# Sines and exponentials by three groups in turn, with a third buffer for their arguments, and the order of all tasks searched anew

## The chip, the core and the metric

The kernel runs on one core of one Trainium2 chip. The metric is the time of one execution on the device in microseconds (us). The engines are named as the profile names them: PE (TensorE, matrix products into PSUM; PEld are its weight loads), DVE (VectorE), ACT (ScalarE, which evaluates functions from a loaded table), POOL (GpSimd) and SP (SyncE, which here only issues DMAs). Each engine runs its own instructions in order and waits for others by semaphores.

## The reference

A gate mixes two branches over the same input x (2048 positions, 640 channels):

```python
g = _sigmoid((x * gate_w).sum(-1, keepdims=True))
a = _A_ref(x, A_wqkv, A_wo)
b = _B_ref(x, B_A_re, B_A_im, B_B_re, B_B_im, B_C_re, B_C_im, B_log_dt, B_Dskip)
return g * a + (1 - g) * b
```

Branch A is attention with 32 heads of 20 channels, in which a position looks at 8 positions, 2 apart: q, k and v are x @ wqkv, then a softmax over 8 products of q with k, the weighted sum of v, and a product with wo. Branch B is a state space model with 192 complex states for each of 640 channels. Its convolution kernel is a sum of complex exponentials,

```python
P = jnp.exp(logdA[:, :, None] * l[None, None, :])
K = jnp.einsum("dn,dnl,dn->dl", Cc, P, dB).real
```

over 2048 positions l, and K is convolved with x by Fourier transforms of twice the length.

## The kernel before

One program holds both branches; its instructions are interleaved so that PE, DVE and ACT all have work.

**Order.** The program is written as tasks (`pl.add`), each with an engine or a choice of engines, what it depends on, and the slots it takes and gives back. The order in which tasks are written out, and the engine of each that has a choice, stand in a long string of numbers, `ORDER["main"]` for everything up to the Fourier transform of K and `ORDER["tail"]` for the rest. It was found by a search. An engine's instructions stand in the program in this order and run in it.

**The generator of K** (`KGen`). The 640 channels are taken in ten groups (c = 0 to 9). Of each group, a complex exponential is made from sines and real exponentials of arguments that are linear in l, factored over l. PE makes the arguments (tile `ar`, two buffers in PSUM) from the group's parameters (`L`, the arguments' left side) and a constant (`Rarg`). ACT makes three units of sines for a group (three instructions each) and three units of exponentials (two instructions each) into rings of slots: five slots for sines (`trg`), six for exponentials (`exq`), both parts of the tile `big`, but for one slot in `bufA`. DVE multiplies a unit's sines and exponentials (two instructions to `pt`, one to `qq`, which gives the slots back), and PE sums the products over states (`kps`). A copy to `E` ends a group; after group 4 and group 9 DVE spreads half of K out (`X`), and SP and POOL store it to DRAM (`Kx`) and load it back (`kc`).

Sines and exponentials need different tables in ACT; changing the table is an instruction of its own (ACT_TABLE_LOAD). Before, the groups go in the order sines of 0, exponentials of 0 and 1, sines of 1 and 2, exponentials of 2 and 3, and so on: two of a kind in turn. `L` has two buffers, group c in buffer c mod 2, and the load of group c (eight small DMAs on SP; for group 0 four of them on ACT) waits for the arguments of group c - 2. The parameters behind L (`Sprm` in DRAM) are stored piece by piece from `pc`, by SP or POOL. POOL clears the L buffers at the start.

**Attention** runs in eight rounds of 256 positions (0 to 7). DVE multiplies q with shifted k (`prod`, five instructions of 128 x 2048), PE sums them (`lg`), DVE takes a maximum (`mx`, `hi`, `lo`), ACT an exponential (`at` from `lg`, with the table of exponentials), PE a sum, DVE the quotient (`rs`, `at`). SP stores it to DRAM (`aS`) and loads it back in another layout (`asb`). POOL loads v's window (`vc`). DVE multiplies v with the weights (`pv`, five instructions of 128 x 2048), PE sums (`tb`), a copy goes to `oT`, PE multiplies with wo, and a scaled copy (`ga`) is stored (`gaS`). The copies out of PSUM (`oT`, `ga`, projections to `qA`, `kA`, `prj`, `vst`, `pv`; `big` and `bufA` from `bp` and `tb`) can run on ACT or DVE, as the order says.

**The rest.** Fourier transforms of x (`Usb` to `big`) and of K (`kc` to `bufA`) are products on PE (`bp`), whose results ACT or DVE copy out. The tail multiplies the spectra (`fp`, copies to `sp_u` and `sp_k`, then DVE's `ta`, `tc`, `Y`), transforms back (`cp`, `yp`) and mixes with branch A (`tt`, `ot`).

Of the kernel before, what the change touches and what calls it, by code (L numbers as in the profile page):

```python
# [11 lines left out]
ALU = mybir.AluOpType  # L12
# [8 lines left out]
S = 2048  # L21
# [19 lines left out]
def _attn_consts():  # L41
# [49 lines left out]
), "tail": (  # L91
# [442 lines left out]
HC = NCH // 2  # L534
CH = 2 * HC * CQ

# [223 lines left out]
class KGen:  # L760
    def __init__(self, cst, pre, tc, prm):
        self.tc, self.nc, self.prm = tc, tc.nc, prm
        nc = tc.nc
        self.Lb = []
        for i in range(2):
            L = pre.tile([128, 2, 2, 2 * NST], BF16, name=f"L{i}", tag="PHI", bufs=3)
            nc.gpsimd.memset(L[:], 0.0)
            for g2 in range(2):
                nc.gpsimd.memset(L[64 * g2:64 * g2 + 2], 1.0)
            self.Lb.append(L)  # L770
        self.R = cst.tile([128, SW + EW], BF16, name="Rarg")
        nc.gpsimd.dma_start(self.R[:], nc.inline_tensor(_arg_consts(), name="c_rarg").ap())
        self.S12 = cst.tile([128, 2, 128], BF16, name="S12")
        nc.gpsimd.dma_start(self.S12[:], nc.inline_tensor(_shift_consts(), name="c_s12").ap())
# [10 lines left out]
    def load_L(self, c, gs=(0, 1)):  # L785
        L = self.Lb[c % 2]
# [8 lines left out]
    def plan(self, pl, pa, pk, hold, params, opened, fin):  # L795
        nc, R = self.nc, self.R
        SCL = float(2.0 * np.pi / 65536.0)
        argt, prevarg, prevact, prevkmm, fins, ns = [], None, None, None, [], 0
        self.pqs, self.lastargs = [], argt
        for c in range(NCH):  # L800
            L = self.Lb[c % 2]
            if c:
                Lt = [pl.add(f"L{c}", "S", 5.2, lambda _, c=c: self.load_L(c), deps=argt[c - 2] if c > 1 else params, dma=1.3)]
            else:
                Lt = [pl.add(f"L0{e}", e, d, lambda _, g=g: self.load_L(0, (g,)), deps=params, dma=0.65) for g, e, d in ((0, "S", 1.5), (1, "A", 1.7))]
            argt.append([])
            ends, held = {}, {}
            b = {"started": set()}
            for kind in (0, 1) if c % 2 == 0 else (1, 0):
                for u in range(3):  # L810
                    ends[u, kind] = []
                    for gp in range(2):
                        for sub in ((0, 1) if gp == 0 else (0,)) if kind == 0 else (None,):
                            def args(_, u=u, kind=kind, gp=gp, sub=sub, b=b, L=L):
                                ar = b["ar"] = pa.tile([128, 2, 512], F32, name="ar")
# [619 lines left out]
```

## Time and profile before

| | us |
|---|---|
| runs (three) | 320.24, 322.25, 322.69 |
| median of the runs | 322.25 |
| the profiled execution | 319.85 |
| its span, first to last instruction | 318.1 |
| ACT busy, of the span | 290.8 |
| DVE busy | 289.6 |
| PE busy | 289.2 |

The profile describes one execution; its own time is below all three runs, and sums from it are made against 319.85 us. A row of the timeline reads: start, length, engine, line, operation, what is written from what, shapes, count, and in brackets the idle time ahead and what ended it. An engine with a q behind its name (SPq, ACTq) is its queue of DMA issues, and a length there is the time of issuing, not of the transfer. Rows of groups read: line, engine, operation, tiles, shapes, count | busy us in all, mean ns of one | idle us ahead. Rows of stages read: start:end, length, and the busy us of PE, PEld, DVE, ACT and POOL with their counts of instructions, then the granted clock, the share of DMA and GB/s. Instructions of ACT and DVE that follow one another overlap a little, so that a row's start to the next row's start is what an instruction takes from its engine's time.

### The profile page before, as it was taken

The page shows a single profiled execution, that of the slowest core. Times are in us where ns is not written, and L with a number is a line of the kernel's source. Part 1 is how long each engine was busy: PE and PEld are TensorE (multiplying, and loading weights), DVE is VectorE, ACT ScalarE, POOL GpSimd, SP SyncE. Part 2 cuts the span into 40 slices and gives each one's busy share as a digit, 9 for nine tenths or more (in the row PEclk, how much of TensorE's full clock was granted, in tenths as well). Part 3 has the DMA queues.
Part 4 walks back from the last instruction along what each step waited for, and adds up shares of the span by engine and source line. Part 5 has one row for each costly group of instructions (what it writes and reads, how often), then busy time and mean ns, then how long its engine had stood idle before and what let it go on. Part 6 is the DMA issues. An engine that isn't in the chain of part 4 may idle for free. (4 is left out here: it accounts for less than half of the span.)

```text
span 318.1 us, 12105 instructions
## 1 busy us (share of the span) xinstructions
PE 289.2 (91%) x5276; PEld 171.2 (54%) x5276; DVE 289.6 (91%) x401; ACT 290.8 (91%) x431; POOL 57.4 (18%) x87
## 2 busy tenths in 40 slices
PE   8899989989999999999988999989989999997860
PEld 3545543445555454546454555546657776667740
DVE  4999989999899999999999999998867799999891
ACT  3999959998999999999999999998998999997891
POOL 8710211551000001111032122030020000000063
PEclk9999999999999999999999999978999999997995
DMA  8994655574612114534687696751195436874057
GB/s 254 365 251 116 167 157 113 139 149 117 130 19 68 34 45 112 135 64 128 218 222 187 130 231 144 132 126 35 46 313 205 154 116 187 184 144 68 2 140 194
DMA packets 48494, 45.67 MB, mean 144 GB/s; under 512 B 28490, under 2 KB 42106, under 8 KB 48442
## 3 DMA queue, kind: packets, MB, share of 16 engines
q1 hardware_dynamic: 42088, 27.17, 33.5%
q0 software_dynamic: 5392, 17.01, 20.9%
q8 instruction: 41, 0.67, 0.9%
q10 hardware_dynamic: 962, 0.73, 0.9%
q14 instruction: 11, 0.09, 0.1%
HBM read 29.57 MB, written 14.01 MB: 137 GB/s over the span
## 5 line engine op out<-in xcount | busy, mean ns | idle before, releaser
L316 PE MATMUL tb<-bufA 128*128 128x512 bf16 x300 | 75.5, 383 | 2.6 <-ACT bufA L513 1.3
L843 ACT ACTIVATE big<-ar 128x740 bf16<-128x740 int16 (+1 forms) x72 | 57.2, 859 | 0.9 <-PE ar L828 0.6
L828 PE MATMUL ar<-Rarg,L 64*128 64x212 bf16 (+4 forms) x600 | 48.2, 255 | 4.2 <-ACT big L843 1.6
L845 ACT ACTIVATE big<-ar 128x848 bf16<-128x848 f32 x60 | 50.2, 909 | 0.2 <-PE ar L828 0.2
L316 PEld LDWEIGHTS <-bufA 128*128 128x128 bf16 x300 | 31.5, 120 | 29.4 <-issue 9.6
L455 DVE TENSOR_TENSOR pv<-vc,asb 128x2048 bf16<-128x2048 bf16 x40 | 47.3, 1216 | 0.0
L828 PEld LDWEIGHTS <-L 64*128 64x128 bf16 x600 | 20.8, 95 | 34.1 <-issue 31.1
L865 DVE TENSOR_TENSOR pt<-big 128x1024 bf16<-128x1024 bf16 x48 | 32.2, 700 | 0.5 <-ACT big L843 0.5
L883 PEld LDWEIGHTS <-pt 128*32 128x32 bf16 (+1 forms) x2560 | 23.1, 92 | 13.3 <-issue 10.9
L883 PE MATMUL kps<-qq,pt 128*32 128x21 bf16 (+1 forms) x2560 | 28.0, 175 | 1.5 <-issue 1.5
L486 PE MATMUL tb<-wo_sb,oT 128*128 128x320 bf16 x160 | 27.7, 301 | 0.0
L381 DVE TENSOR_TENSOR prod<-qA,kA 128x2048 bf16<-128x2048 bf16 x20 | 23.7, 1216 | 0.4 <-PE lg L387 0.4
L381 DVE TENSOR_TENSOR prod<-prj 128x2048 bf16<-128x2048 bf16 x20 | 23.8, 1217 | 0.0
L462 PE MATMUL tb<-pv,ind 128*64 128x512 bf16 (+1 forms) x192 | 22.6, 359 | 1.2 <-DVE prj L515 1.1
L513 ACT ACTIVATE sp_u<-fp 128x640 bf16<-128x640 f32 x31 | 22.0, 811 | 0.7 <-PE fp L1096 0.7
L867 DVE TENSOR_TENSOR qq<-big 128x1344 bf16<-128x1344 bf16 x24 | 21.2, 882 | 0.0
L513 ACT ACTIVATE sp_k<-fp 128x640 bf16<-128x640 f32 x30 | 21.0, 819 | 0.0
L374 POOL DMA_DIRECT2D vc<-vS x16 | 11.6, 729 | 50.4 <-DVE pv L455 36.4
L1214 POOL DMA_DIRECT2D out_dram<-ot x14 | 7.7, 558 | 69.3 <-PE yp L1187 67.2
L1096 PEld LDWEIGHTS <-PHI 128*128 128x128 bf16 x160 | 15.6, 97 | 7.7 <-issue 0.9
L486 PEld LDWEIGHTS <-oT 128*128 128x128 bf16 x160 | 13.3, 98 | 7.4 <-issue 3.2
L513 ACT ACTIVATE big<-bp 128x1024 bf16<-128x1024 f32 x15 | 15.0, 1044 | 2.1 <-PE bp L1327 2.1
(177 smaller groups left out, 539.9 us busy)
## 6 DMA issues: line engine op xcount, KB each, us to landing
vc<-vS POOLq DMA_DIRECT2D x16, 327.5 KB, 5.5
gaS<-ga SPq DMA_DIRECT2D x8, 320.0 KB
Usb<-in_A_x_dram POOLq DMA_DIRECT2D x8, 320.0 KB, 5.3
gaF<-gaS SPq DMA_DIRECT2D x8, 320.0 KB
bufA<-in_A_wqkv_dram SPq DMA_DIRECT2D x3, 800.0 KB
L<-Sprm SPq DMA_DIRECT2D x76, 30.0 KB
asb<-aS SPq DMA_DIRECT2D x16, 128.0 KB
psi<-c_psi SPq DMA_DIRECT2D x4, 512.0 KB
```

The lines of the kernel that those rows point to most:

```text
L316: nc.tensor.matmul(ppf, self.wq[:, which, kt, e::5], self.xT[:, c0 // 1024, kt, c0 % 1024:c0 % 1024 + SC], start=(kt == 0), stop=(kt == NK ...
L381: nc.vector.tensor_tensor(b[e][:], q[:, e, o:o + C].unsqueeze(1).to_broadcast([128, W, C]), win(k[:, e, :], o, W, DIL, C), ALU.mult)
L455: nc.vector.tensor_tensor(o, vw, b["asb"][:].unsqueeze(2).to_broadcast(sh), ALU.mult)
L462: nc.tensor.matmul(b["op", e][64 * a:64 * a + 64, 0:n, :], ind[:, 32:96], b["pv", e][:, w, a, 0:n, :], start=(w == 0), stop=(w == 3), skip ...
L486: nc.tensor.matmul(apf[:, :320], b["oT"][:, e, i * 128:(i + 1) * 128], wo_sb[:, e, hf * 320:(hf + 1) * 320], start=(e == 0), stop=(e == 4))
L513: nc.scalar.activation(o, i, ACT.Identity)
L828: nc.tensor.matmul(ar[:, g2, a0:a0 + ncol], L[rows, sb, gv, l0:l0 + 128], R[rows, c0:c0 + ncol], start=True, stop=True, tile_position=(64 ...
L843: nc.scalar.activation(d_[:, :, s0 * QW:s1 * QW], ar[:].bitcast(I16)[:, :, 0:2 * (s1 - s0) * QW:2], ACT.Sin, scale=SCL)
L845: nc.scalar.activation(dst[:, gp::2].rearrange("p g s n -> p g (s n)"), ar[:, :, 0:2 * EW], ACT.Exp)
L865: nc.vector.tensor_tensor(pt[:, :, k, :], gg[:, :, ::-1] if k else gg, e1, ALU.mult)
L867: nc.vector.tensor_tensor(qq[:], trg[:, :, KI:].rearrange("p a (v m) -> p a v m", v=2), exq[:, :, KI:].unsqueeze(2).to_broadcast([128, 32, ...
L883: nc.tensor.matmul(kps[32 * g:32 * g + 32, h, NM * ql:NM * ql + NM], pt[rows, k, v, :], qq[rows, k, v, :], start=(g not in started), stop= ...
```

## The change

Three things are changed by hand, and the order of tasks is new.

Groups go by threes: a list `KINDS` of (group, kind), kind 0 for sines and 1 for exponentials, replaces the pairwise alternation. It reads sines of 0; exponentials of 0, 1, 2; sines of 1, 2, 3; exponentials of 3, 4, 5; sines of 4, 5, 6; exponentials of 6, 7, 8; sines of 7, 8, 9; exponentials of 9. The rings keep five and six slots. `L` gets a third buffer, in a pool that had three slots already, and the load of group c waits for the arguments of group c - 3. And the tail's `mx` may run on POOL too; the new order doesn't use that.

```diff
+KINDS = [(c, k) for g in range(0, NCH, 3) for k, cs in ((0, (g - 2, g - 1, g)), (1, (g, g + 1, g + 2))) for c in cs if 0 <= c < NCH]
...
-        for i in range(2):
+        for i in range(3):
             L = pre.tile([128, 2, 2, 2 * NST], BF16, name=f"L{i}", tag="PHI", bufs=3)
             nc.gpsimd.memset(L[:], 0.0)
...
-        L = self.Lb[c % 2]
+        L = self.Lb[(c + 2) % 3]
...
-                Lt = [pl.add(f"L{c}", "S", 5.2, lambda _, c=c: self.load_L(c), deps=argt[c - 2] if c > 1 else params, dma=1.3)]
+                    Lt_[c] = [pl.add(f"L{c}", "S", 5.2, lambda _, c=c: self.load_L(c), deps=argt[c - 3] if c > 2 else params, dma=1.3)]
...
-            for kind in (0, 1) if c % 2 == 0 else (1, 0):
+        for c, kind in KINDS:
...
+            if len(ends) < 6:
+                continue
...
-            os = pl.add(f"mx{n}", "D", 0.06 + 0.167 * w, mix, deps=[v])
+            os = pl.add(f"mx{n}", "DG", {"D": 0.06 + 0.167 * w, "G": 0.25 + 0.7 * w}, mix, deps=[v])
...
-    "14 -14 2 1 3 -5 3 3D 47 -46 47 -3 1 -3 1 11 1 5 1 -59 1 53 -59 4 13 36 -31D 1G 42 -41 42 1 1 -61 1 43 1D 8 1 1 -52 44D "
+    "54 -40 41 -3 1 -3 1 11 -62 1 1 2 3D -2 5 53 1 -61 3 5 63 -66 1 66 1 -54 7D 1G -3 38 1 -54 55 -7 -4 1D 20 1 1D 4 1 -71 "
```

What the new order moves shows at three places. The rows are instructions in the order in which they stand on one engine; x2 counts two alike, and the numbers behind names tell buffers apart.

First, ACT, around the exponential of attention's round 4 (`at` from `lg`; L843 and L845, now L844 and L846, are the generator's sines and exponentials). Before:

```order
L843 ACTIVATE bufA<-ar 128x2x444
L843 ACTIVATE bufA<-ar 128x2x370 x2
L415 ACT_TABLE_LOAD
L415 ACTIVATE at<-lg 128x512
L845 ACTIVATE big<-ar 128x2x424 x2
L513 ACTIVATE vst<-tb 128x512 x2
```

and now:

```order
L844 ACTIVATE bufA<-ar 128x2x444
L844 ACTIVATE bufA<-ar 128x2x370
L415 ACT_TABLE_LOAD
L415 ACTIVATE at<-lg 128x512
L844 ACT_TABLE_LOAD
L844 ACTIVATE bufA<-ar 128x2x370
L844 ACTIVATE big<-ar 128x2x444
L513 ACTIVATE oT<-tb 128x512
L844 ACTIVATE big<-ar 128x2x370 x2
```

Attention's exponential stood where the generator changed from sines to exponentials, and shared that load; now it stands within a stretch of sines, with a load on either side. Over the whole program ACT has 18 loads before and 19 now.

Second, DVE, from the softmax of the last round (`at`, round 7) to its first products with v (the `pv` of the block's last rows). Before:

```order
L424 TENSOR_TENSOR at_5054<-at_5054,rs_5217 128x512
L455 TENSOR_TENSOR pv_101<-vc_5051,asb_5214 128x4x512 x2
L865 TENSOR_TENSOR pt_5233<-big_617 128x32x32 x2
L867 TENSOR_TENSOR qq_5234<-big_617 128x1344
L455 TENSOR_TENSOR pv_101<-vc_5051,asb_5214 128x4x512 x2
L455 TENSOR_TENSOR pv_101<-vc_5051,asb_5214 128x8x256
L865 TENSOR_TENSOR pt_5312<-big_617 128x32x32 x2
L867 TENSOR_TENSOR qq_5313<-big_617 128x1344
L865 TENSOR_TENSOR pt_5388<-bufA_78,big_617 128x32x32 x2
L867 TENSOR_TENSOR qq_5389<-bufA_78,big_617 128x1344
L455 TENSOR_TENSOR pv_101<-vc_4716,asb_5407 128x4x512 x2
```

and now:

```order
L424 TENSOR_TENSOR at_5229<-at_5229,rs_5263 128x512
L868 TENSOR_TENSOR pt_5267<-big_628 128x32x32 x2
L870 TENSOR_TENSOR qq_5268<-big_628 128x1344
L868 TENSOR_TENSOR pt_5374<-big_628 128x32x32 x2
L497 TENSOR_SCALAR ga_5399<-tb_5312,g_sb_65 128x320
L870 TENSOR_TENSOR qq_5375<-big_628 128x1344
L497 TENSOR_SCALAR ga_5399<-tb_5402,g_sb_65 128x320
L868 TENSOR_TENSOR pt_5418<-bufA_78,big_628 128x32x32 x2
L870 TENSOR_TENSOR qq_5419<-bufA_78,big_628 128x1344
L497 TENSOR_SCALAR ga_5399<-tb_5436,g_sb_65 128x320
L455 TENSOR_TENSOR pv_101<-vc_5282,asb_5588 128x4x512 x2
```

The five `pv` of round 6 stood between the two (the rows with `asb_5214`); they now stand ahead of this softmax, and three `ga` have come in. From the softmax of round 6 to those `pv` of round 6, now:

```order
L424 TENSOR_TENSOR at_4767<-at_4767,rs_4828 128x512
L868 TENSOR_TENSOR pt_4897<-big_628 128x32x32 x2
L870 TENSOR_TENSOR qq_4898<-big_628 128x1344
L868 TENSOR_TENSOR pt_4902<-big_628 128x32x32
L381 TENSOR_TENSOR prod_5081<-qA_1871,kA_1872 128x2048
L868 TENSOR_TENSOR pt_4902<-big_628 128x32x32
L870 TENSOR_TENSOR qq_4903<-big_628 128x1344
L403 TENSOR_REDUCE mx_5148<-lg_4907 128x64
L406 TENSOR_SCALAR hi_5150<-mx_5148 128x64
L407 SCALAR_TENSOR_TENSOR lo_5151<-mx_5148,hi_5150 128x64
L455 TENSOR_TENSOR pv_101<-vc_4687,asb_5064 128x4x512 x4
```

(two more `prod` follow the one shown). Before, those `pv` came only behind the softmax of round 7.

Third, DVE, at the first products of the generator (group 0, units 0 to 2). Before:

```order
L865 TENSOR_TENSOR pt_805<-big_617 128x32x32 x2
L867 TENSOR_TENSOR qq_806<-big_617 128x1344
L865 TENSOR_TENSOR pt_924<-big_617 128x32x32 x2
L867 TENSOR_TENSOR qq_925<-big_617 128x1344
L865 TENSOR_TENSOR pt_929<-big_617 128x32x32
L455 TENSOR_TENSOR pv_101<-vc_657,asb_936 128x4x512
L865 TENSOR_TENSOR pt_929<-big_617 128x32x32
L867 TENSOR_TENSOR qq_930<-big_617 128x1344
```

and now:

```order
L868 TENSOR_TENSOR pt_828<-big_628 128x32x32 x2
L870 TENSOR_TENSOR qq_829<-big_628 128x1344
L868 TENSOR_TENSOR pt_839<-big_628 128x32x32 x2
L870 TENSOR_TENSOR qq_840<-big_628 128x1344
L868 TENSOR_TENSOR pt_959<-big_628 128x32x32 x2
L455 TENSOR_TENSOR pv_101<-vc_546,asb_757 128x4x512 x4
L423 RECIPROCAL rs_993<-lg_711 128x64
L424 TENSOR_TENSOR at_845<-at_845,rs_993 128x512
L870 TENSOR_TENSOR qq_960<-big_628 128x1344
```

The `qq` of unit 2, which gives its slots back, now comes behind four `pv` and the end of a softmax.

The evictions also change engine: ACT gives up four `ga` and three `sp_u` and takes one `sp_k`, one `big`, one `bufA` of 1024 columns for one of 512, and one `bufA` from `tb`; DVE the other way round. POOL stores five pieces of `Sprm` in place of three.

More of the change, by code (lines that the diff above doesn't have):

```diff
@@ L797, in plan @@
         SCL = float(2.0 * np.pi / 65536.0)
[L798 removed]
+        prevarg, prevact, prevkmm, fins, ns = None, None, None, [], 0
+        argt, ends_, held_, b_, Lt_ = [[] for _ in range(NCH)], {}, {}, {}, {}
         self.pqs, self.lastargs = [], argt
[L800 to L855 removed]
@@ new lines, in plan, with args, act @@
+        for c, kind in KINDS:
+            L = self.Lb[(c + 2) % 3]
+            if c not in b_:
+                if c:
+                    Lt_[c] = [pl.add(f"L{c}", "S", 5.2, lambda _, c=c: self.load_L(c), deps=argt[c - 3] if c > 2 else params, dma=1.3)]
+                else:
+                    Lt_[c] = [pl.add(f"L0{e}", e, d, lambda _, g=g: self.load_L(0, (g,)), deps=params, dma=0.65) for g, e, d in ((0, "S", 1.5), (1, "A", 1.7))]
+                ends_[c], held_[c], b_[c] = {}, {}, {"started": set()}
+            Lt, ends, held, b = Lt_[c], ends_[c], held_[c], b_[c]
+            for u in range(3):
+                ends[u, kind] = []
+                for gp in range(2):
+                    for sub in ((0, 1) if gp == 0 else (0,)) if kind == 0 else (None,):
+                        def args(_, u=u, kind=kind, gp=gp, sub=sub, b=b, L=L):
+                            ar = b["ar"] = pa.tile([128, 2, 512], F32, name="ar")
+                            runs, a0 = [], 0
+                            if kind == 0:
+                                s0, s1 = UNITS[2 * gp + sub]
+                                for x in range(s0 // 4, (s1 + 3) // 4):
+                                    q0, q1 = max(s0 - 4 * x, 0), min(s1 - 4 * x, 4)
+                                    runs.append((x // 2, x % 2, q0 * QW, (q1 - q0) * QW))
+                            else:
+                                runs = [(gp, 0, SW, EW), (gp, 1, SW, EW)]
+                            for gv, sb, c0, ncol in runs:
+                                for g2 in range(2):
+                                    rows = slice(64 * g2, 64 * g2 + 64)
+                                    l0 = 128 * (2 - u if gv else u)
+                                    nc.tensor.matmul(ar[:, g2, a0:a0 + ncol], L[rows, sb, gv, l0:l0 + 128], R[rows, c0:c0 + ncol],
+                                                     start=True, stop=True, tile_position=(64 * g2, 0))
+                                a0 += ncol
+                            b["ar", u, kind, gp, sub] = ar
+                        def act(_, u=u, kind=kind, gp=gp, sub=sub, b=b):
+                            opened()
+                            ar = b.pop(("ar", u, kind, gp, sub))
+                            if gp == 0 and not sub:
+                                b["T", u, kind] = self.ring[kind][self.turn[kind] % len(self.ring[kind])]
+                                self.turn[kind] += 1
+                            dst = b["T", u, kind]
+                            if kind == 0:
+                                s0, s1 = UNITS[2 * gp + sub]
+                                d_ = dst.rearrange("p g s n -> p (g s n)").rearrange("p (g x) -> p g x", g=2)
+                                nc.scalar.activation(d_[:, :, s0 * QW:s1 * QW], ar[:].bitcast(I16)[:, :, 0:2 * (s1 - s0) * QW:2], ACT.Sin, scale=SCL)
+                            else:
+                                nc.scalar.activation(dst[:, gp::2].rearrange("p g s n -> p g (s n)"), ar[:, :, 0:2 * EW], ACT.Exp)
+                        first = not ends[u, kind]
+                        a = pl.add(f"arg{c}{kind}{u}{gp}{sub}", "P", ((0.205, 0.17)[min(2 * gp + (sub or 0), 1)], 0.193)[kind], args, deps=Lt, after=[prevarg] + ([self.moved] if c == HC + 2 else []), acq=["ar"], eq=(SW, 2 * EW)[kind])
+                        t = pl.add(f"act{c}{kind}{u}{gp}{sub}", "A", ((0.79, 0.67)[min(2 * gp + (sub or 0), 1)], 0.762)[kind], act, deps=[a], after=[prevact] + (hold if first and kind == 0 and ns == NTR - 1 else []), acq=[("trg", "exq")[kind]] if first else [],
+                                   rel=[("ar", a)], table=("sin", "exp")[kind])
+                        if first:
+                            held[u, kind] = t
+                            ns += kind == 0
+                        prevarg, prevact = a, t
+                        argt[c].append(a)
+                        ends[u, kind].append(t)
+            if len(ends) < 6:
+                continue
@@ L1193, in scale, with mix @@
                 nc.scalar.activation(t[:, k].rearrange("p (r d) -> p r d", r=2), q["yp", n][:, :, 160 * k:160 * k + 160], ACT.Identity, scale=om32[:, u:u + 1])
-        def mix(_, n=n, us=us, w=w, o=o, k0=k0):
-            nc.vector.tensor_tensor(q["ot", o][:, k0:k0 + w], q["tt", n][:, 0:w], gaF[:, us[0]:us[0] + w], ALU.add)
+        def mix(e, n=n, us=us, w=w, o=o, k0=k0):
+            {"D": nc.vector, "G": nc.gpsimd}[e].tensor_tensor(q["ot", o][:, k0:k0 + w], q["tt", n][:, 0:w], gaF[:, us[0]:us[0] + w], ALU.add)
         def both(_, n=n, us=us, o=o, k0=k0):
```

39 lines of the change are left out of this document (removed), and 84 rows, old and new, of the table ORDER.

## The prediction

> **What bounds the kernel now.** I read the page's first part, then the engines by stages, then the waits of each engine, and last the timeline at the places that the new order touches.
>
> The page's line of busy times:
>
> ```profile
> PE 289.2 (91%) x5276; PEld 171.2 (54%) x5276; DVE 289.6 (91%) x401; ACT 290.8 (91%) x431; POOL 57.4 (18%) x87
> ```
>
> Three engines are equally full, so no single one can be relieved with profit. The stages (start:end, length, then busy time of PE, weight loads, DVE, ACT, POOL) say where there is room:
>
> ```profile
> 36.00:60.00 24.00, 22.11 (x176) 9.77 (x176) 22.05 (x34) 20.06 (x29) 5.02 (x8) 1.00 0.51 131
> 60.00:220.00 160.00, 153.33 (x3569) 82.79 (x3567) 155.47 (x208) 156.92 (x233) 26.76 (x41) 0.98 0.53 125
> 220.00:250.00 30.00, 28.11 (x473) 20.66 (x471) 23.89 (x36) 26.91 (x37) 2.84 (x5) 1.00 0.48 164
> 250.00:300.00 50.00, 47.20 (x574) 35.22 (x572) 47.24 (x69) 47.38 (x73) 0.00 (x0) 0.97 0.54 127
> ```
>
> From 60 to 220 us, where sines, exponentials and attention run together, ACT idles 160 - 156.92 = 3.1 us and DVE 4.5 us. An order can win at most that there, and lose any amount. Idle time worth having lies at 36 to 60 (ACT 3.9, DVE 2.0), at 220 to 250 (DVE 6.1, ACT 3.1) and at 250 to 300 (2.8 and 2.6).
>
> **The change, part by part.**
>
> *Table loads.* The timeline of ACT (start, length, what) at a switch from sines to exponentials:
>
> ```profile
> 52.56 2.38 ACT L843 ACTIVATE big<-ar 128x888 bf16<-128x888 int16 x3
> 54.95 1.28 ACT L845 ACT_TABLE_LOAD   x1
> 56.25 1.65 ACT L845 ACTIVATE big<-ar 128x848 bf16<-128x848 f32 x2
> 57.78 0.60 ACT L415 ACTIVATE at<-lg 128x512 bf16<-128x512 f32 x1
> 58.26 1.67 ACT L845 ACTIVATE big<-ar 128x848 bf16<-128x848 f32 x2
> ```
>
> A switch costs 1.28 us. Sines and exponentials by themselves switch ten times before and seven times after, which would save 3 x 1.28 = 3.9 us. But the eight exponentials of attention use the exponential's table too, and in longer stretches of sines more of them fall among sines: as the order's rows show, one now stands between two loads. Counted over the whole of ACT's order, there are 18 loads before and 19 after: **+1.28 us of ACT**, no gain. [...]
>
> *Evictions dealt out anew.* No other work is added. Copies out of PSUM change engine; groups by shape (busy us, mean ns | idle ahead):
>
> ```profile
> L513 ACT ACTIVATE sp_u<-fp 128x640 bf16<-128x640 f32 x31 | 22.0, 811 | 0.7 <-PE fp L1096 0.7
> L513 ACT ACTIVATE big<-bp 128x1024 bf16<-128x1024 f32 x15 | 15.0, 1044 | 2.1 <-PE bp L1327 2.1
> L495 ACT ACTIVATE ga<-tb,g_sb 128x320 bf16<-128x320 f32 x26 | 14.9, 595 | 0.5 <-PE tb L486 0.3
> L515 DVE CAST big<-bp 128x1024 bf16<-128x1024 f32 x5 | 6.0, 1220 | 3.9 <-PE bp L1327 3.9
> L497 DVE TENSOR_SCALAR ga<-tb,g_sb 128x320 bf16<-128x320 f32 x6 | 3.3, 544 | 0.4 <-issue 0.3
> ```
>
> ACT gives up four ga (4 x 14.9/26 = 2.3) and three sp_u (2.1), takes one sp_k (0.7, of the same size), one big (1.0), smaller ones of some 1.2 by the same view, and the table load (1.3): -0.2. DVE takes four ga (2.2) and three sp_u (2.4; one is 0.82, in the last fence below) and gives up one sp_k (0.8), one big (1.2) and 1.6 of smaller ones: +1.0. Both engines are full, so the end moves by something between the mean of the two (+0.4) and DVE's own: **+0.7**.
>
> *The last two rounds of attention.* This is the step that I trust least. DVE ends the softmax (at), SP stores it to DRAM (aS, four DMAs), waits until that has landed, loads it back spread out (asb, two DMAs), and DVE's products pv need it. DVE's queue is in order: a pv that waits holds the generator's products behind it, and those hold the slots that ACT writes to. DVE and SP before:
>
> ```profile
> 195.61 0.69 DVE L424 TENSOR_TENSOR at<-at,rs 128x512 bf16<-128x512 bf16 x1
> ...
> 209.18 0.69 DVE L424 TENSOR_TENSOR at<-at,rs 128x512 bf16<-128x512 bf16 x1
> 209.79 2.35 DVE L455 TENSOR_TENSOR pv<-vc,asb 128x2048 bf16<-128x2048 bf16 x2
> 212.06 1.32 DVE L865 TENSOR_TENSOR pt<-big 128x1024 bf16<-128x1024 bf16 x2
> 213.29 0.88 DVE L867 TENSOR_TENSOR qq<-big 128x1344 bf16<-128x1344 bf16 x1
> 214.10 3.49 DVE L455 TENSOR_TENSOR pv<-vc,asb 128x2048 bf16<-128x2048 bf16 x3
> ...
> 220.48 1.33 DVE L865 TENSOR_TENSOR pt<-bufA,big 128x1024 bf16<-128x1024 bf16 x2 [0.86 <-ACT bufA L843]
> 221.73 0.88 DVE L867 TENSOR_TENSOR qq<-bufA,big 128x1344 bf16<-128x1344 bf16 x1
> 222.53 2.35 DVE L455 TENSOR_TENSOR pv<-vc,asb 128x2048 bf16<-128x2048 bf16 x2
> ```
>
> ```profile
> 196.32 2.54 SPq L429 DMA_DIRECT2D aS<-at  x4
> 204.28 1.17 SPq L434 DMA_DIRECT2D asb<-aS  x2
> 208.57 0.39 SPq L507 DMA_DIRECT2D gaS<-ga  x1
> 209.90 2.53 SPq L429 DMA_DIRECT2D aS<-at  x4
> 215.59 1.17 SPq L434 DMA_DIRECT2D asb<-aS  x2
> ```
>
> Round 6: at ends at 196.30, asb is issued by 205.45 (9.15 later), pv starts at 209.79 (13.5 later) without a wait. Round 7: 209.87, 216.76 (6.9 later), 222.53 (12.7 later). Between them DVE had other work. In the new order less stands between. For round 7 it is three units of the generator's products (212.06 to 214.10 = 2.04 each) and three ga (0.54 each): 7.7 us. For round 6 it is two units, three prod (as large as pv: 212.06 - 209.79 = 2.27 for two, 1.13 each) and the maximum with its two small followers (an estimate, 1.1): 8.6 us. How long asb takes to land after its issue isn't shown; it is above 0 and at most 209.79 - 205.45 = 4.3 us. The nearest row of a landing is a result's store, in the chain of waits:
>
> ```profile
> 305.15 2.03 DMA out_dram<-ot
> ```
>
> With 2.0 us, pv would wait 9.15 + 2.0 - 8.6 = 2.6 us in round 6 and 6.9 + 2.0 - 7.7 = 1.2 in round 7. Part of it replaces waits that are there already (DVE waited 0.86 us for the last sine at 220.48), so I take half: **+2.0**, between 0 and 8.4 (landing in 4.3 us: 4.9 and 3.5). [...]
>
> *The slots of the exponentials.* Three groups in a row are nine units for a ring of six. The ninth unit can only be written when DVE has finished the third unit's qq, and the order's rows show this qq behind four pv and the next softmax. From the rows above and these:
>
> ```profile
> 57.93 1.33 DVE L865 TENSOR_TENSOR pt<-big 128x1024 bf16<-128x1024 bf16 x2
> ```
>
> DVE reaches the end of that qq at 57.93 + 2 x 2.04 + 1.24 (two pt, 212.06 to 213.29) + 4 x 1.13 + 1.2 (at from 209.18 to 209.79, its reciprocal likewise) + 0.8 = 69.8. ACT comes to the ninth unit after 16 exponentials (56.25 to 57.78 is two, 0.76 each), one of attention's (57.78 to 58.26, 0.48) and five evictions of the same size: 56.25 + 12.2 + 2.9 = 71.3. The margin is 1.5 us, here and at the three later stretches like it; before, two groups of six units fill the ring just once. **+0.3**, between 0 and 4 x 1 us.
>
> *The third buffer.* Its memsets go to POOL, ahead of the constants and of POOL's first Sprm store:
>
> ```profile
> 3.06 2.72 POOL L767 MEMSET L<- 128x1536 bf16 x2
> 5.69 5.64 POOL L769 MEMSET L<- 2x1536 bf16 x4
> 16.11 0.84 POOL L674 DMA_DIRECT2D Sprm<-pc  x1 [2.25 <-DVE pc L729]
> ```
>
> ```profile
> 41.01 5.93 SPq L793 DMA_DIRECT2D L<-Sprm  x12
> ...
> 58.29 4.43 SPq L793 DMA_DIRECT2D L<-Sprm  x8
> ```
>
> Half as much again is 4.2 us. POOL idled 2.25 us ahead of that store, so this piece is stored 1.9 us later. What needs it is the first load of L at 41.01, behind the pieces made last, 23 us on. Cost 0; if that cover were gone, up to 2 us. On SP, group 2's load of L moves up behind asb of round 0, where the load in that place started at 58.29 and took 4.4 us to issue. Its first use comes after 12 exponentials and five others of 0.48, at 56.25 + 9.1 + 2.4 = 67.8, so 5 us remain for landing: cost 0, bound +2. The later loads gain room.
>
> *Waits that go.* At the start of the last stage DVE waited for PE, and at 45 us ACT for PE:
>
> ```profile
> 252.64 0.82 DVE L515 CAST sp_k<-fp 128x640 bf16<-128x640 f32 x1 [1.96 <-PE fp L1096]
> 45.32 0.60 ACT L513 ACTIVATE vst<-tb 128x512 bf16<-128x512 f32 x1 [1.21 <-PE tb L316]
> ```
>
> The new order gives DVE the first two sp_u, and PE computes those ahead of that sp_k: **-1.0** (0 to -2). It gives ACT one vst instead of two: **-0.5** (0 to -1.2).
>
> **Sum.** 0.7 + 2.0 + 0.3 - 1.0 - 0.5 = +1.5 us. The profiled execution took 319.85 us (span 318.1 and 1.75 around it): 321.35 for its counterpart. The other runs took 320.24, 322.25 and 322.69; the mean of all four, 321.26, lies 1.4 above the profiled one. I put the forecast at 321.35 + 1.4 = **322.8 us**: no change that counts.
>
> **Rivals.**
>
> 1. *Faster: the new order closes gaps that I can't see from counts.* If it takes half of ACT's idle time at 36 to 60, 220 to 250 and 250 to 300 (3.9 + 3.1 + 2.6 = 9.6, half 4.8) and the waits of attention don't arise, the sum is 0.7 - 4.8 = -4.1: about 317.2 us. For it: all three engines idle in these stages, so the cause is order, not work. Against it: at 220 to 250 ACT's work is hardly changed, and the middle has nothing to give. Chance 0.20.
>
> 2. *Slower: asb takes the place of the waits removed.* If asb lands 4.3 us after its issue, pv waits 4.9 us in round 6 and 3.5 in round 7; nothing is absorbed, and the sum is 1.5 - 2.0 + 8.4 = +7.9: 329.2 us. It decides against the forecast from the point at which the two waits cost 2.7 us more than my 2.0 (325.5 us): unabsorbed, that is a landing of 2.5 us. For it: aS itself took 5.4 us to land in round 6. Against it: pv never waited before, so 4.3 is only an upper end. Chance 0.17.
>
> 3. *Slower: ACT held by the ring.* If DVE runs late by 2.5 us at the four places, the margin of 1.5 is gone and each costs ACT 1.0, and DVE again when the next sines come late; +4 with that: 326.5 us. For it: both directions are now tight, since DVE still waits for ACT's sines (0.86 at 220.48). Against it: a wait that costs one engine time gives the other slack at the next place. Chance 0.13.
>
> **Chances and range.** About 1%, or 3.2 us, is what a measurement tells from no change here: faster is below 319.0, slower above 325.5. Faster 0.20 (rival 1), slower 0.30 (rivals 2 and 3), same 0.50 (the forecast). The range takes in the terms' bounds and half of rivals 1 and 2: 318.5 to 328.
>
> **What would show it.** Table loads: 19, with ACT's busy time within 1 us of 290.8; DVE's at 290.6. Attention: in the last two rounds a wait of pv for a DMA or asb, 1 to 3 us each; none means that term was wrong. Ring: an idle ACT ahead of an exponential that was released by DVE's qq. Tail: the 1.96 us at its start mostly gone. The forecast is wrong if ACT's idle time from 60 to 220 grows by more than 3 us, or if that at 220 to 300 falls by more than 3.

## The result and the profile after

| | before | after |
|---|---|---|
| median of 20 runs each, us | 322.29 | 323.96 |
| lowest and highest | 320.03, 324.67 | 321.85, 326.19 |
| the profiled execution, us | 319.85 | 325.39 |
| its span | 318.1 | 323.6 |

The ratio of after to before is 1.0077 (95% interval 1.0054 to 1.0100): 2.5 us slower, a small loss that 20 runs can tell and that lies under the 1% which the prediction counted as a change. The profiled execution of after is one of its slower ones, so the 5.5 us between the two profiles overstate the loss.

The stages of after (columns as before; those of the kernel before stand in the prediction):

```profile
36.00:60.00 24.00, 23.54 (x172) 10.59 (x172) 22.21 (x35) 20.13 (x29) 4.90 (x8) 1.00 0.71 159
60.00:220.00 160.00, 153.22 (x3587) 83.17 (x3584) 155.75 (x210) 157.89 (x234) 27.26 (x42) 1.00 0.53 123
220.00:250.00 30.00, 25.57 (x435) 16.89 (x432) 18.99 (x33) 23.23 (x29) 2.28 (x4) 0.83 0.39 135
250.00:300.00 50.00, 46.26 (x484) 33.58 (x484) 48.65 (x71) 46.74 (x75) 0.00 (x0) 1.00 0.57 142
```

From 60 to 220 us nothing is lost: ACT idles 2.1 us, 3.1 before. At 220 to 250 all three engines do less in the same 30 us: DVE 18.99 for 23.89, ACT 23.23 for 26.91, PE 25.57 for 28.11. And of these four rows it is the one with a granted clock below 1.00: 0.83.

DVE around the last round's first pv, in after:

```profile
222.44 0.89 DVE L870 TENSOR_TENSOR qq<-bufA,big 128x1344 bf16<-128x1344 bf16 x1
223.24 0.55 DVE L497 TENSOR_SCALAR ga<-tb,g_sb 128x320 bf16<-128x320 f32 x1
226.16 2.36 DVE L455 TENSOR_TENSOR pv<-vc,asb 128x2048 bf16<-128x2048 bf16 x2 [2.38 <-DMA asb<-aS]
228.44 0.50 DVE L515 CAST E<-kps 128x336 bf16<-128x336 f32 x1
```

and PE in the same microseconds:

```profile
226.65 0.66 PE L1334 MATMUL bp<-F1k,kc 128*128 128x256 bf16 x4
229.00 0.65 PE L925 MATMUL nxp<-E,S 128*128 128x320 bf16 x4 [1.70 <-DVE E L515]
229.58 1.06 PE L462 MATMUL tb<-pv,ind 128*64 128x512 bf16 x4
```

The wait that the prediction named is there: pv waits 2.38 us for asb. Behind pv stands E, the last group's copy, and PE, whose next instruction is nxp from E, stands still for 1.70 us. The timeline row behind it shows what follows: four tb at 1.06 us, which take 0.62 us at a clock of 1.00 (in the run without that wait, below).

Round 6 waits 0.28 us. In this execution round 0 waits too, 2.38 us at 66.08; in eight later profiles with the same order up to there that pv starts at 63.61 to 63.86 us, so a wait there belongs to an execution and not to the order.

### The profile page after: what moved, and what is told of

Its sections match the earlier page's. It is cut to its first block, busy times and chain, and to the rows that moved or that the text cites. A ratio compares the mean times of both kernels' runs of the same rounds, so it can differ in the third digit from the quotient of the medians.

```text
span 323.6 us, 12105 instructions
## 1 busy us (share of the span) xinstructions
PE 289.9 (90%) x5276; PEld 169.5 (52%) x5276; DVE 291.1 (90%) x405; ACT 291.2 (90%) x428; POOL 63.2 (20%) x92
## 4 chain that ended last, share of the span: by engine, by line
PE 36%; DVE 24%; ACT 18%; DMA 13%; issue 4%; SPq 2%; POOL 1%; ACTq 0%; POOLq 0%; DVEq 0%
PE tb L316 10%; PE ar L829 7%; DVE pv L455 5%; DMA asb<-aS 4%; PE kps L886 4%; PE tb L486 4%; ACT bufA L513 4%; DMA aS<-at 4%; PE tb L462 3%; DMA L<-Sprm 3%; DVE tc L1127 3%; DVE Y L1130 2%; PE lg L387 2%; ACT big L844 2%; ACT sp_u L513 2%
## 5 line engine op out<-in xcount | busy, mean ns | idle before, releaser
L316 PE MATMUL tb<-bufA 128*128 128x512 bf16 x300 | 76.7, 390 | 2.6 <-ACT bufA L513 1.3
L844 ACT ACTIVATE big<-ar 128x740 bf16<-128x740 int16 (+1 forms) x72 | 56.4, 850 | 1.4 <-PE ar L829 1.2
L846 ACT ACTIVATE big<-ar 128x848 bf16<-128x848 f32 x60 | 50.8, 923 | 1.2 <-DVE qq L870 0.3
L829 PE MATMUL ar<-Rarg,L 64*128 64x212 bf16 (+4 forms) x600 | 47.3, 252 | 4.3 <-ACT big L844 2.7
L462 PE MATMUL tb<-pv,ind 128*64 128x512 bf16 (+1 forms) x192 | 24.8, 371 | 0.5 <-DVE pv L455 0.4
L513 ACT ACTIVATE sp_k<-fp 128x640 bf16<-128x640 f32 x31 | 23.4, 961 | 1.2 <-PE fp L1099 1.2
L374 POOL DMA_DIRECT2D vc<-vS x16 | 11.6, 729 | 41.0 <-DVE pv L455 35.9
```

The lines of the kernel that those rows point to most:

```text
L316: nc.tensor.matmul(ppf, self.wq[:, which, kt, e::5], self.xT[:, c0 // 1024, kt, c0 % 1024:c0 % 1024 + SC], start=(kt == 0), stop=(kt == NK ...
L462: nc.tensor.matmul(b["op", e][64 * a:64 * a + 64, 0:n, :], ind[:, 32:96], b["pv", e][:, w, a, 0:n, :], start=(w == 0), stop=(w == 3), skip ...
L513: nc.scalar.activation(o, i, ACT.Identity)
L829: nc.tensor.matmul(ar[:, g2, a0:a0 + ncol], L[rows, sb, gv, l0:l0 + 128], R[rows, c0:c0 + ncol], start=True, stop=True, tile_position=(64 ...
L844: nc.scalar.activation(d_[:, :, s0 * QW:s1 * QW], ar[:].bitcast(I16)[:, :, 0:2 * (s1 - s0) * QW:2], ACT.Sin, scale=SCL)
L846: nc.scalar.activation(dst[:, gp::2].rearrange("p g s n -> p g (s n)"), ar[:, :, 0:2 * EW], ACT.Exp)
```

## The experiments

Each ran in five rounds beside the kernel before on its chip, and every ratio is to that. Four theories stood against one another. **1**: the waits of pv for asb hold E and X and make the loss. **2**: the added work makes it. **3**: the stage from 220 us on is bound by PE's bp. **4**, formed after the first four runs: the wait costs little; PE's gap behind it lowers PE's clock, and that costs.

The table sums them up. The last three columns are from each run's profile: from the start of the last softmax (at) to E, from E to the first tb of the second half's transform (tb from kc), and the granted clock in that second stretch. In the two rows of before's main part (before; before, new tail), at to E holds round 6's five pv, 5.8 us, which stand ahead of at in the others.

| kernel | ratio (95% interval) | at to E | E to tb | clock |
|---|---|---|---|---|
| before | 1 | 16.82 | 18.08 | 1.00 |
| after | 1.0077 (1.0054 to 1.0100) | 12.84 | 20.20 | 0.75 |
| after, again | 1.0066 (1.0025 to 1.0107) | 12.92 | 19.16 | 0.82 |
| wo load later | 1.0200 (1.0131 to 1.0270) | 13.12 | 19.33 | 0.81 |
| no wait of pv in round 7 | 1.0002 (0.9968 to 1.0035) | 11.30 | 16.77 | 1.00 |
| two table loads less | 1.0116 (1.0074 to 1.0158) | 13.46 | 19.51 | 0.74 |
| tail of before | 1.0120 (1.0080 to 1.0159) | 13.01 | 20.19 | 0.75 |
| pv behind X | 1.0165 (1.0114 to 1.0215) | 11.63 | 23.92 | 0.75 |
| and kps earlier | 1.0281 (1.0228 to 1.0334) | 11.52 | 26.43 | 0.70 |
| PE busy, 12 products | 1.0016 (0.9979 to 1.0054) | 13.27 | 17.93 | 0.90 |
| PE busy, 24 products | 0.9998 (0.9973 to 1.0023) | 13.38 | 16.81 | 1.00 |
| nxp later | 1.0039 (1.0006 to 1.0072) | 13.20 | 16.89 | 1.00 |
| before, new tail | 1.0017 (0.9988 to 1.0047) | 15.71 | 18.08 | 1.00 |
| 24 products, old tail | 0.9977 (0.9941 to 1.0013) | 12.93 | 16.82 | 1.00 |

The clock in the table is one execution's. For every run the mean granted clock over the whole kernel is on record too, and it says the same: its median is 0.964 to 0.969 in the two series of after, 0.971 to 0.979 in those of before that ran beside the experiments, and 0.980 in each of no wait of pv in round 7, 24 products and nxp later.

**The wo load later.** On POOL:

```diff
 omS store
-wo_sb<-in_A_wo_dram x2
 vS<-vst
 Dk<-in_B_Dskip_dram x8
+wo_sb<-in_A_wo_dram x2
 vc<-vS x2
```

> The kernel after, with one load moved on POOL's queue: attention's output matrix wo (800 KB) is loaded behind the Dk loads (issue at about 65 us) instead of ahead of them (47.6 us). Theory 1 (the waits of pv for asb make the loss, and the one of round 0 comes from this load, which is on the wire while round 0's weights go out and come back): asb of round 0 lands in time, the 2.4 us that DVE waits at 66 us are gone, and 1.2 to 2.4 us of them reach the end: 321.6 to 322.8 us, no longer to be told from the kernel before (ratio 0.998 to 1.002). Theory 2 (the loss is the added work: one table load of 1.28 us and 1.0 us of evictions on DVE; waits are absorbed): time as after, 323.5 to 324.5 (ratio 1.004 to 1.007), whether the wait goes or not. Theory 3 (the loss arises from 220 us on, where PE runs at a granted clock of 0.83 and ACT and DVE wait for its bp): as theory 2, with the wait gone.

Measured 1.0200, against all three. Round 0's pv doesn't wait (63.63, right behind its forerunner), but it doesn't in most profiles with the load early either. What was lost shows on PE; its timeline:

```profile
73.29 0.18 PE L886 MATMUL kps<-qq,pt 128*32 128x21 bf16 x4
76.38 0.37 PE L886 MATMUL kps<-qq,pt 128*32 128x21 bf16 x28 [2.92 <-issue]
```

PE stops for 2.92 us in the middle of one task's products, with nothing to wait for ("issue"), while the moved load and its neighbours keep the DMAs at a share of 1.04 (70 to 78 us; 0.43 to 0.47 in after). Its granted clock is lowered there as well, 0.74 from 74 to 78 us. The run says nothing on theory 1; whether the moved load makes the stop was not tried.

**No wait of pv in round 7.**

```diff
+                if sc == 6:
+                    self.asb6 = b["asb"]
...
-nc.vector.tensor_tensor(o, vw, b["asb"][:]...
+nc.vector.tensor_tensor(o, vw, (self.asb6 if sc == 7 else b["asb"])[:]...
```

> The kernel after, but the products pv of attention's last round take the weights asb of the round before (round 7's weights are still made, stored and loaded, and not used), so that DVE doesn't wait there for a DMA. Theory 1: the 2.4 us of waiting at 226 us are gone, E and X of the last half come 2 us earlier, and the time falls by 1.2 to 2.4 us to 321.6 to 322.8 (ratio 0.998 to 1.002). Theory 2: DVE waits for something else there instead and the time stays within 0.5 us of 324.0. Theory 3: DVE is not what the stage from 220 us waits for, PE's bp is; time within 0.5 us of 324.0, with the waits for bp as long as in after (7.2 us on DVE, 4.7 on ACT) or longer.

Measured 1.0002: the whole loss is gone. PE in this run:

```profile
226.40 0.65 PE L927 MATMUL nxp<-E,S 128*128 128x320 bf16 x4
226.98 0.62 PE L464 MATMUL tb<-pv,ind 128*64 128x512 bf16 x4
```

No gap ahead of nxp, and tb at 0.62. Theory 1 gets its fall, and theory 3, which expected none here, falls itself. But from E on, where pv waits for no DMA in either kernel, this run is 3.4 us shorter than after (16.77 for 20.20) with the same instructions in the same order, and the clock is 1.00 for 0.75. That a wait doesn't explain, and theory 4 came from it.

**Two table loads less.**

```diff
-ACT.Exp, scale=scale)
+ACT.Identity if sc == 4 else ACT.Exp, scale=scale)
```

> The kernel after, but ACT's exponential of attention's round 4 is a plain copy with the same scale, so that round's weights are not a softmax; the table needn't change for it, and two of the 19 table loads (1.28 us each) go. Nothing else moves. Theory 2: ACT is the engine that bounds the stage at 145 us (idle 0.3 us in 60), so both loads come off the end: 2.0 to 2.6 us, 321.4 to 322.0 (ratio 0.997 to 1.000). Theory 1: ACT gets ahead by 2.6 us there and gives it back when it next waits for DVE's qq or PE's ar, since DVE is as busy; 323.0 to 324.0 (ratio 1.002 to 1.006). Theory 3: as theory 1.

Measured 1.0116: ACT has 17 loads for 19 and is 2.5 us less busy (288.7 for 291.2), and the time doesn't fall: the next run, measured together with it and with all 19 loads, gave 1.0120. Theory 2 falls for ACT's part of the work; DVE's part falls with the 24 products, below.

**The tail of before.** The string `ORDER["tail"]` of before in the kernel after.

> The kernel after with the tail's order of before, and the main part's of after. The prediction gave the new tail -1.0 us at its start (DVE and ACT waited 1.96 us there before, 0.88 after) less about 0.3 for evictions that change engine. If that is right: 0.5 to 1.0 us slower than after, 324.5 to 325.0 (ratio 1.007 to 1.009). If the tail costs, and not the main part: 321.5 to 323 (ratio 0.998 to 1.002). Theories 1 and 2 both have the loss in the main part, so neither expects it to fall.

Measured 1.0120. Beside after's 1.0077, measured at another time, that looks like the predicted gain of the new tail. But the run of two table loads less, with the new tail and measured together with this one, gave 1.0116. It decides nothing; the run of before with the new tail does.

**After, again**, as the measure for the next three.

> The kernel after, unchanged, on the chip of the three runs beside it, as their measure. Expected: ratio to the kernel before of 1.005 to 1.010, a wait of pv for asb of 2 to 3 us in the last round, and none in round 0, since of the runs so far with this place of the wo load only one profiled execution had it (there the four stores of round 0's weights took 4.34 us to issue, 2.60 to 2.77 in the others).

As expected: 1.0066, waits of 2.45 us in round 7, none in round 0, and 0.81 in round 6.

**pv behind X**, and **kps earlier** besides. On DVE and PE:

```diff
 DVE: ga<-tb,g_sb
-DVE: pv<-vc,asb x2
 DVE: E<-kps ... X<-nxt
+DVE: pv<-vc,asb x2
 DVE: pv<-vc,asb x3
 PE: nxp<-E,S
-PE: tb<-pv,ind x8
 PE: bp<-F1c,Usb ...
+PE: tb<-pv,ind x8
```

> The kernel after with one change of order: the first two pv of the last round stand on DVE behind E and X of group 9 instead of ahead of them, and on PE the sums of those two products stand three bp later. All the work is done. Theory 1 (the wait of pv for asb holds E and X, and with them all that follows): E waits for its kps alone and is cast at 226.8 instead of 228.4 (in after's times), asb has landed when pv's turn comes, and the time falls by 1.5 to 3 us to 321 to 322.5 (ratio 0.998 to 1.003). Theory 4 (what costs is less the wait than PE's lowered clock behind it, set off by the gap of 1.70 us in which PE waits for E): the gap shrinks to under 0.8 us, the granted clock from 220 to 250 stays at 0.95 or above, and the fall is the same as with theory 1; the two differ in the next run but one. If neither holds: within 0.5 us of after.

> As the run before it, and besides the last 192 products kps of group 9 stand on PE ahead of two bp instead of behind them, so that E needn't wait for evictions of bp: E at about 224.5 in after's times, X 3 us earlier than in after. If the chain from E over X, its store and its load to the last half's transform sets the end, as theory 1 has it: 2.5 to 4 us less than after, 320 to 321.5 (ratio 0.994 to 1.000). If the stage is bound by bp and its evictions instead, no more than the run before it: ratio 0.998 to 1.003.

Measured 1.0165 and 1.0281: worse, though E came sooner (11.6 us behind at). I had moved the tb too far, behind the fifth pv, which is written into the buffer of the first; so in both runs the first products' sums read the fifth's, and the last round's outputs aren't the reference's. PE waits for that pv, here in pv behind X:

```profile
231.23 0.54 PE L1330 MATMUL bp<-F1c,Usb 64*128 64x128 bf16 x8 [0.38 <-ACT big L513]
235.64 1.92 PE L462 MATMUL tb<-pv,ind 128*64 128x512 bf16 x8 [3.87 <-DVE pv L455]
```

Neither tests the order that I meant. They do show the stretch behind E growing to 23.92 and 26.43 us with PE's gap and a clock of 0.75 and 0.70.

**PE busy, 12 products.**

```diff
 nx = X["nx"] = psp.tile([128, 2, 512], F32, name="nxp", tag="ar")
+for k in range(12 if hf else 0):
+    nc.tensor.matmul(nx[:, 0, 0:256], S12[:, 0], S12[:, 0:2]..., start=True, stop=True)
```

> The kernel after, with 12 more products of 128x128 by 128x256 on PE ahead of nxp of the second half (on constants, into nxp's own buffer, which nxp then overwrites), where PE waits 1.70 us for E: PE is busy there, and DVE's wait, E and X stay where they were. Theory 4: the granted clock stays at 0.95 or above from 228 to 248 (0.57 to 0.90 in after) and the time falls by 1.5 to 2.7 us to 321.3 to 322.5 (ratio 0.998 to 1.003). Theory 1: the clock may stay up, the time doesn't follow: 323.5 to 324.5 (ratio 1.005 to 1.009).

Measured 1.0016; after itself, measured together with it, 1.0066. The intervals overlap, so by the times alone it is open; the profile shows a shorter stretch at a higher clock (17.93 us, 0.90), with DVE's wait no shorter than in after (2.80 us for 2.38).

**PE busy, 24 products**: three more ahead of each of the bp (fu) 11, 4, 19 and 10.

```diff
+if name == "fu" and n in (11, 4, 19, 10):
+    z = pk.tile([128, 2, 256], F32, name="kps", tag="kb")
+    for k in range(3):
+        nc.tensor.matmul(z[:, 0], kg.S12[:, 0], kg.S12[:, 0:2]..., start=True, stop=True)
```

> As the run with 12 more products ahead of nxp, and three more ahead of each of four later bp (into the buffer of kps, which is free by then), 24 in all, so that PE has no long gap in the stage after E. DVE still waits for asb and E comes as late as in after. Theory 4 (the lowered clock, not the wait, is the larger part): the granted clock stays at 1.00 from E to the first tb of the second half, that stretch takes 16.5 to 17.5 us, as in the run without the wait (16.77), instead of 19 to 20, and the time comes 2 to 3 us below after: ratio 0.997 to 1.001. Theory 1 (the wait and what it holds back): the stretch is bound by evictions and by E's lateness and stays at 18 to 19 whatever the clock; ratio 1.002 to 1.006.

Measured 0.9998. DVE in this run:

```profile
225.80 2.36 DVE L455 TENSOR_TENSOR pv<-vc,asb 128x2048 bf16<-128x2048 bf16 x2 [2.92 <-DMA asb<-aS]
228.07 0.50 DVE L515 CAST E<-kps 128x336 bf16<-128x336 f32 x1
```

and PE:

```profile
226.78 1.47 PE L923 MATMUL nxp<-S 128*128 128x256 bf16 x12
228.63 0.64 PE L927 MATMUL nxp<-E,S 128*128 128x320 bf16 x4 [0.38 <-DVE E L515]
229.19 0.62 PE L462 MATMUL tb<-pv,ind 128*64 128x512 bf16 x4
```

pv waits longer than in after (2.92 for 2.38), E is as late, PE has 24 products more to do, and the loss is gone. The work that the change added to ACT and DVE is all still there, so theory 2 falls as a whole; what theory 4 says of the clock holds. The stretch from E to tb as the view of stages has it, first after, then this run:

```profile
228.44:248.64 20.20, 17.48 (x176) 10.23 (x177) 11.56 (x23) 14.30 (x18) 2.28 (x4) 0.75 0.48 170
```

```profile
228.07:244.88 16.81, 16.15 (x190) 10.57 (x189) 11.56 (x23) 13.90 (x18) 2.28 (x4) 1.00 0.58 204
```

DVE's work is the same 11.56 us, ACT's within 0.4, PE has more products and is busy for less time. Against after the fall is 1.0077 - 0.9998 = 0.0079 (0.0034 either way, from the two intervals): 2.5 us, all of the loss.

**nxp later**, on PE:

```diff
 bp<-F1k,kc
+tb<-pv,ind x8 (with bp<-F1c,Usb between)
 nxp<-E,S
-tb<-pv,ind x8 (with bp<-F1c,Usb between)
```

> The kernel after with one change of order, all its work done: on PE the two tb of the last round's first pv and one bp stand ahead of nxp instead of behind it (and that bp's eviction on ACT ahead of nxt), so that PE has something to do while E is late; DVE's order is unchanged, and it waits for asb as in after. Theory 4: PE's gap of 1.70 us goes, the clock stays up, the stretch from E to the first tb of the second half is 16.5 to 18 us instead of 19 to 20, and the time comes 1.5 to 3.5 us below after: ratio 0.996 to 1.002. Theory 1: the wait is on DVE and stays, E, X and their load come no earlier: within 0.7 us of after, ratio 1.005 to 1.009.

Measured 1.0039, with the stretch at 16.89 us and a clock of 1.00. The profile is theory 4's, and the change adds no work; the ratio lies between the two theories' ranges. Why it is above the 24 products' (the intervals overlap) is open.

**Before, new tail.** `ORDER["tail"]` of after in the kernel before.

> The kernel before with the tail's order of after. The prediction's term: 1.0 us less for the start of the tail, less some tenths for evictions that change engine, ratio 0.995 to 0.998. Against it: in the profiles so far the time from the first tb of the second half to the end was 74.02 us with the old tail in before and 74.46 with it in the run of after with the old tail, and 74.5 to 75.4 with the new one, which gives nothing or a loss: ratio 1.000 to 1.003.

Measured 1.0017 (0.9988 to 1.0047): no gain of 1.0 us or more. Why, DVE's timeline at the start of the tail shows, first with the old tail in after:

```profile
256.30 0.82 DVE L515 CAST sp_k<-fp 128x640 bf16<-128x640 f32 x1 [2.56 <-PE fp L1099]
257.23 0.83 DVE L1127 TENSOR_TENSOR ta<-sp_u,sp_k 128x1280 bf16<-128x1280 bf16 x1
```

then after, again, with the new one:

```profile
253.53 1.56 DVE L515 CAST sp_u<-fp 128x640 bf16<-128x640 f32 x2 [0.87 <-PE fp L1099]
255.16 0.82 DVE L515 CAST sp_k<-fp 128x640 bf16<-128x640 f32 x1
256.08 0.82 DVE L1127 TENSOR_TENSOR ta<-sp_u,sp_k 128x1280 bf16<-128x1280 bf16 x1
```

The wait shrinks from 2.56 to 0.87, and two copies of together 1.6 us fill the place. The first product ta comes 9.49 us behind tb (247.74) in the one, 9.42 (246.66) in the other. It is the same in the kernel before and in this run: the wait falls from 1.96 to 0.28 us, and ta comes 9.48 and 9.43 us behind tb.

**24 products, old tail**, the best that these runs point to.

> The main part of after with the 24 products more on PE, as two runs before, and the tail's order of before: what the runs so far point to as the best of both. With those products and the new tail the ratio was 0.9998; the new tail on the kernel before gave 1.0017 (0.9988 to 1.0047). If the new tail is the loss of 0.0017 that this says, the ratio is 0.997 to 0.999; if the tail makes no difference, 0.999 to 1.001. If the prediction's gain for the new tail is there after all (1.0 to 1.5 us) and only hidden in that run, 1.002 to 1.006.

Measured 0.9977 (0.9941 to 1.0013): not to be told from before.

## Why the prediction was right, and where its steps were not

The forecast, 322.8 us and no change that counts, held: 323.96 in the median, inside the range. That the sum came out near is luck, as its terms show.

- **The last two rounds, +2.0.** The place and the wait were right, the path to the end wrong. The prediction put half of the waits on the end because "a pv that waits holds the generator's products behind it". In round 7 those are through; behind pv stands E, and PE waits for E. The wait itself, kept in the run with 24 products, costs nothing that can be told (0.9998 with it, 1.0002 without; some 1.4 us either way). In the profiles it does reach tb: 30.19 us behind at with the wait, 28.07 without. How much of it is absorbed behind that stays open. What costs is PE's lowered clock in the stretch behind E (0.75 for 1.00): 2.5 us, by the run with 24 products. The gap that the wait makes on PE goes ahead of that drop in after; it is not the only thing that brings one (last section). The sizes: 2.38 to 2.99 us in round 7, for 1.2 estimated, and 0 to 0.8 in round 6, for 2.6. Round 6 came out small because asb was issued 1.5 us behind the end of aS's issue (202.68 to 204.21); the 5.4 us of before (198.86 to 204.28), which the estimate took over, didn't recur. The landing was underrated at 2.0 us: pv began 3.2 us behind the end of asb's issue in round 7 and 3.9 in round 6, each as soon as asb was there.

```profile
200.14 2.54 SPq L429 DMA_DIRECT2D aS<-at  x4
204.21 1.18 SPq L434 DMA_DIRECT2D asb<-aS  x2
...
221.75 1.17 SPq L434 DMA_DIRECT2D asb<-aS  x2
```

- **Waits that go, -1.0 and -0.5.** The waits went as foreseen (1.96 to 0.88 us, 1.21 to 0.24), the gain didn't. In the tail, copies took their place; at 36 to 60 us ACT idles 3.87 us, 3.94 before. A wait on one engine was counted as time off the end without asking what that engine does with it.
- **Table loads and evictions, +0.7.** The counts held: 19 loads, ACT busy 291.2 (forecast 290.8), DVE 291.1 (290.6). Two loads less gained nothing, so ACT's part of the price was not on the path.
- **The ring, +0.3.** Right: the longest wait of ACT for qq is 0.31 us. The margin of 1.5 held.
- **The third buffer, 0.** Not tried by itself. POOL is busy 5.8 us longer (63.2 for 57.4), and up to 220 us ACT and DVE idle no longer than before (13.3 us for 13.8, and 10.6 for 11.7).
- **Rivals.** Rival 2 needed asb to land in 4.3 us; it came to 3.2 to 3.9, beyond the 2.5 at which that rival was to decide against the forecast. Its price was too high all the same: round 6 hardly waited, and the wait of round 7 by itself cost nothing that can be told. Rivals 1 and 3 didn't come. What the prediction's tests left out was the direction that came true: ACT's idle time at 220 to 300 grew, by 4.3 us.

So two gains of together 1.5 that never came, a work term of 0.7 whose ACT part was free, and a wait of 2.0 stood against a clock loss of 2.5 that was no term at all.

## What to carry to other kernels

Before pricing a wait, follow it to PE: if it leaves PE with gaps just ahead of a stage of matrix products (here 1.70 us, with 0.75 behind it), read the granted clock of the stage behind it in fine windows. A few useless products into a free buffer, or independent ones moved ahead of the late one, cost little there (ratios of 0.9998 and 1.0039 for 1.0077 without) and show whether the clock is the loss. And a wait that goes is a gain only if the next thing that this engine hands on comes earlier (ta came 9.48 us behind tb with the wait of 1.96, 9.43 with 0.28).

## What was not expected of the hardware

PE's clock was lowered behind gaps of 1.70 us (after) and 1.75 us (after, again), and the drop came 0 to 6 us behind them. PE in after, again, by stretches of 2 us (busy time, count, granted clock, share of DMA, GB/s):

```profile
226.00:228.00 2.00, 0.25 (x3) 1.00 0.04 8
228.00:230.00 2.00, 1.94 (x20) 1.00 0.00 0
230.00:232.00 2.00, 1.42 (x23) 1.00 0.40 145
232.00:234.00 2.00, 1.62 (x24) 1.00 1.06 370
234.00:236.00 2.00, 2.00 (x22) 0.53 0.38 141
236.00:238.00 2.00, 1.87 (x24) 0.62 0.87 185
238.00:240.00 2.00, 1.29 (x19) 1.00 1.00 415
240.00:242.00 2.00, 1.70 (x18) 0.74 1.01 384
242.00:244.00 2.00, 2.00 (x19) 0.50 0.18 74
```

The gap ahead of nxp is at 226 to 228 (PE idles 1.75 us of the 2), a clock of 0.53 at 234 to 236, and of 0.50 at 242 to 244. In after itself the drop comes right behind the gap of 1.70 us: 0.90 at 228 to 230, 0.50 at 230 to 232.

But such a gap isn't needed. In the run with two table loads less, PE is slow already ahead of its gap of 1.19 us (nxp there starts at 227.44):

```profile
222.53 0.54 PE L1330 MATMUL bp<-F1c,Usb 64*128 64x128 bf16 x8 [0.20 <-ACT big L513]
223.45 1.00 PE L1334 MATMUL bp<-F1k,kc 128*128 128x256 bf16 x4 [0.38 <-ACT big L513]
```

The same four bp take 0.60 us in after (225.67). The run with the later wo load has it likewise (1.01 us, at 229.62). With 12 products more the clock is 0.50 at 240 to 242, with no gap longer than 0.48 us from 222 us on. And the kernel before has a drop of its own, in the main part, behind a gap of 0.79 us:

```profile
208.00:210.00 2.00, 1.13 (x88) 1.00 0.52 37
210.00:212.00 2.00, 1.57 (x52) 0.67 0.77 226
212.00:214.00 2.00, 2.00 (x16) 0.50 0.68 141
```

The same place in before with the new tail, which has the same order up to there, keeps its clock:

```profile
210.00:212.00 2.00, 0.95 (x80) 1.00 0.35 32
212.00:214.00 2.00, 1.57 (x57) 1.00 0.85 245
214.00:216.00 2.00, 1.79 (x18) 1.00 0.65 128
```

So the runs show that the clock was the loss and that filling PE kept it up (0.75 and a ratio of 1.0077 in after, 1.00 and 0.9998 with the 24 products); how much idle time lowers it, and when, stays open.

PE also stopped where nothing that the profile shows is waited for: 2.92 us in the run with the later wo load, and 2.47 us in that with kps earlier, both in runs of small kps products. Whether it waited there for instructions was not tried. The DMA view of the run with the later wo load counts the packets of the instruction queue, their MB and their share of time, but not when they came:

```profile
q8 instruction: 41, 0.67, 0.9%
```

What ended the two stops stays open.
